# Delta-rule attention with two expert layers on one core: odd head pairs on the other half of the partitions, eight low weight parts offered to GpSimd, one chunk's turned keys in a gate tile

## The chip, the cores and the metric

The kernel runs on one core of a Trainium2 chip. What counts is the device time of one execution in microseconds (us), and of several executions the median. Engines are named as the profile names them: PE (TensorE, matrix products), PEld (its weight loads), DVE (VectorE), ACT (ScalarE), POOL (GpSimd) and SP (which starts the transfers).

## The reference

```python
# B, H, S, D = 4, 8, 768, 48
k_n = k / (norm(k, axis=-1) + 1e-6)
for t in range(S):                       # per batch and head, state is 48 x 48
    y[t] = q[t] @ state                  # read before the update
    v_old = k_n[t] @ state
    state = state + beta[t] * outer(k_n[t], v[t] - v_old)
x = y as (3072, 384)                     # 8 heads of 48 side by side
h = x @ w_in                             # 384 -> 2048
x = (h * sigmoid(1.702 * h)) @ w_out     # 2048 -> 384
p = domain_probs / (domain_probs.sum(-1) + 1e-9)
out = sum over e of p[:, e] * (relu(x @ w1[e]) @ w2[e])   # 4 experts, 384 -> 1024 -> 384
```

## The kernel before

**Attention.** The 768 tokens are cut into 12 chunks of 64 (u = 0 to 11). The 32 heads of all batches form 16 pairs (g = 0 to 15); x = 0 or 1 is the head in its pair. Of a pair, what lies by the feature sits on partitions `DR[x]` (0 and 64 on, 48 of each) and what lies by the token on `TR[x]` (64 and 0 on, 64 of each). A chunk takes these PE steps, each for all pairs: the key gram (L526 and L530, in `queue_g`), the query gram (L454, in `queue_q`), the old values `ks` (L750), two rounds of `solve` (L760) with a `cross` between (L774), the read of y (L791) and the state's update `write` (L813), the last five in `queue_chain`. A product in f32 stands in the profile as two matmuls, each with its weight load, so 32 products are 64 matmuls.

**Where products lie in the PE array.** Rows are chosen by the partitions of the operands, columns by those of the result. `ks`, both grams and `write` take their operands from one half of the partitions and leave the result on the other half: head x = 0 goes from rows 0 to columns 64, x = 1 from rows 64 to columns 0. `solve` stays on one 32 x 32 block of the diagonal, and four such blocks take turns. The pairs are worked in two halves (g 0 to 7, 8 to 15), each with a PSUM bank of its own (`ch0` and `ch1`, or two of `yg`, `ch0`, `ch1` for the grams, which the profile calls gp), one half after the other.

**Experts.** Tokens of two chunks form a tile of 512. Its first expert layer is L946 (into ph), then the gate on ACT and DVE, then L1043 (into px). The six tiles' first layers fill the PE between the steps of the attention; the second layer (L1170, L1200) follows when the attention is done. Tile 0 needs chunks u = 0 and 1; tile 1 is begun by halves, the first when y of u = 2 has been split (`split_x`, L940).

**What sets the order.** The class `Order` keeps a clock for each engine and a list of tasks with costs, dependencies and priorities. After each matmul of the experts it places the tasks that its clocks say are ready. So the order on every engine is fixed when the program is built, and a changed cost moves instructions. A task whose buffer is not free (`can`) waits; four scratch tiles (scr) are shared.

**Weights of the first layer.** Each of 16 blocks arrives as 64-bit numbers and is made 32-bit (`small` on ACT, `low` and `shift` on DVE), then split into a high part (`hi`, ACT) and a low part (`lo`, DVE, L285). GpSimd sets up masks and later computes the inverses (`queue_inverse`, L584 to L590).

**Turned keys.** Each chunk's keys are turned by DVE (L343) into a scratch tile and copied to kt by 8 copies (L181). For u = 3 the squares of the keys already stand in a tile of the gate's pool (two buffers).

Of the kernel before, what the change touches and what calls it, by code (L numbers as in the profile page):

```python
# [149 lines left out]
def delta_attention_moe_moe_kernel(  # L150
# [72 lines left out]

    def grid(t):
        return t[:, 0:NP * D].rearrange("p (g d) -> p g d", d=D)
# [18 lines left out]
    def queue_w1(f, after):  # L244
# [39 lines left out]
        def lo():  # L284
            nc.vector.tensor_tensor(out=W[f][:, 1, :], in0=cell["t"], in1=W[f][:, 0, :].bitcast(F32), op=ALU.subtract)  # L285
# [7 lines left out]
        wdone[f] = task(lo, "DVE", 0.95, (h,), **kw)  # L293
# [41 lines left out]
    def queue_turn(u, k2t, deps, p):  # L335
# [3 lines left out]
        def turn(h):  # L339
            if h == 0:  # L340
                b = claim(SCR, cell["end"])
                cell["t"] = scr[b][:, 0:NP * C].rearrange("p (h n i) -> p h n i", h=2, i=32)
            V.transpose(out=cell["t"][:, h], in_=k2t[:, 16 * h:16 * h + NP * D].rearrange(  # L343
                "p (g d) -> p g d", d=D)[:, :, 16 * h:16 * h + 32])
# [6 lines left out]
        a = task(lambda: turn(0), "DVE", 0.6, deps, prio=p, can=lambda: any_free(SCR))  # L351
# [80 lines left out]

    def queue_q(u):
# [11 lines left out]
        for g0 in range(0, NP, 8):  # L445
            cell = {}

            def gram(g0=g0, cell=cell):
                ps = cell["ps"] = psa.tile([128, 8, C], F32, name="gp", tag=claim(BANKS, cell["end"]))
                for i in range(8):  # L450
                    g = g0 + i
                    for x in range(2):
                        d = DR[x]
                        mm(ps[TR[x]:TR[x] + C, i, :], lhsT=kt[d:d + D, g, :], rhs=pq[d:d + D, g, x, :],  # L454
                           start=True, stop=True)

            def mask(x, g0=g0, cell=cell):
                r = TR[x]
                V.tensor_tensor(out=pq[r:r + C, g0:g0 + 8, x, :].rearrange("p (g o) i -> p g o i", o=2),
                                in0=cell["ps"][r:r + C].rearrange("p (g o) i -> p g o i", o=2),  # L460
                                in1=pmask[r:r + C].unsqueeze(1).broadcast_to([C, 4, 2, C]), op=ALU.mult)
# [3 lines left out]
            if len(visits) == whole:  # L465
                t = task(lambda fs=tuple(visits): [f() for f in fs], "PE", 1.0 * whole,
# [37 lines left out]
    def queue_g(u):  # L504
# [7 lines left out]
        for g0 in range(0, NP, 8):  # L512
            cell = {}

            def gram(g0=g0, cell=cell):
                ps = cell["ps"] = psa.tile([128, 8, C], F32, name="gp", tag=claim(BANKS, cell["end"]))
                if g0 == 0:
                    G[u] = ap_.tile([128, NP, SB], F32, name="g", tag="g", bufs=4)
                for i in range(8):
                    g = g0 + i  # L520
                    a, b = rows(g)
                    for x in range(2):
                        d, r = DR[x], TR[x] + a
                        for n, o in ((0, a), (SB, b)) if a else ((0, None),):
                            mv = kt[d:d + D, g, :] if o is None else kt[d:d + D, g, o:o + SB]
                            mm(ps[r:r + SB, i, n:n + mv.shape[1]], lhsT=kt[d:d + D, g, a:a + SB], rhs=mv,  # L526
                               start=True, stop=True)
                    for x in range(2):
                        d, r = DR[x], TR[x] + b
                        mm(ps[r:r + SB, i, 0:SB], lhsT=kt[d:d + D, g, b:b + SB], rhs=kt[d:d + D, g, b:b + SB],  # L530
                           start=True, stop=True)

            def keep_d(g0=g0, cell=cell):
                if w not in GG:
                    GG[w] = scr[claim(SCR, gheld[w]["end"])][:, 0:2 * NP * SB].rearrange("p (g i) -> p g i", i=SB)
                gg = GG[w][:, c * NP + g0:c * NP + g0 + 8, :]
                m = gg if w else cmask.unsqueeze(1).broadcast_to([128, 8, SB])
                V.tensor_tensor(out=gg, in0=cell["ps"][:, :, 0:SB], in1=m, op=ALU.mult)

            def keep_x(e, r, o, g0=g0, cell=cell):  # L540
                r += rows(o)[0]
                copy(e, G[u][r:r + SB, g0 + o:g0 + 8:2, :], cell["ps"][r:r + SB, o::2, SB:C])
# [4 lines left out]
            a = task(lambda fs=tuple(h[1] for h in halves): [f() for f in fs], "PE", 0.9 * whole,  # L547
                     (*placed[u], edone.get(u - 4), *diag[-1:]), prio=p, can=lambda: some_free(BANKS, whole))
            first = first or halves[0][0]
            for hc, _, kd, kx in halves:  # L550
                diag.append(task(kd, "DVE", 0.4, (a, premasked.get(w)), prio=p,
                                 can=None if w or u or hc is not first else lambda: any_free(SCR)))
                cross += [task(lambda e, r=r, o=o, kx=kx: kx(e, r, o), ("ACT", "DVE"), (0.24, 0.24), (a,), prio=p + 1)
                          for r in TR for o in range(2)]
                hc["end"] = (diag[-1], *cross[-4:])
# [148 lines left out]
    def queue_chain(u):  # L704
# [15 lines left out]
        def y_free():  # L720
# [6 lines left out]
            if u in YS:  # L727
                return at
# [3 lines left out]
        for hu in range(2):  # L732
            gs = slice(hu * HP, (hu + 1) * HP)
            cell = {}

            def each(gs=gs):
                for i, g in enumerate(range(gs.start, gs.stop)):
# [7 lines left out]
            def ks(take=take, each=each, cell=cell):  # L745
# [6 lines left out]
            def rest(gs=gs, cell=cell):  # L752
                V.tensor_tensor(out=V2[u][:, gs], in0=V2[u][:, gs], in1=cell["ps"], op=ALU.subtract)

            def solve(n, take=take, each=each, cell=cell):
                if u == 0 and n == 0:
                    take()
                for i, g, x in each():
                    r = TR[x] + rows(g)[n]
                    mm(cell["ps"][r:r + 32, i, :], lhsT=Tb[u][r:r + 32, g, :], rhs=V2[u][r:r + 32, g, :],  # L760
                       start=True, stop=True, tile_position=(r, r))

# [13 lines left out]

            def rest2(gs=gs, cell=cell):

                V.tensor_tensor(out=V2[u][:, gs], in0=V2[u][:, gs], in1=cell["ps"], op=ALU.subtract)

            def read(each=each, cell=cell):
                held["yg"] = cell["yev"]
                py = cell["py"] = psa.tile([128, HP, C], F32, name="y", tag="yg")
                for i, g, x in each():
# [6 lines left out]
                    mm(py[o:o + D, i, :], lhsT=SU[:, c0:c0 + D], rhs=pq[:, g, x, :], start=bool(t), stop=True)  # L791

# [17 lines left out]
            def write(each=each, cell=cell):  # L810
                for i, g, x in each():
                    o, r = DR[x], TR[x]
                    mm(cell["ps"][o:o + D, i, :], lhsT=k2[r:r + C, g, :], rhs=SUv[r:r + C, g, x, :],  # L813
                       start=True, stop=True)

            def y_copy(e, x, hu=hu, cell=cell):
                bs, at = slice(hu * B // 2, (hu + 1) * B // 2), slice(DR[x], DR[x] + D)
                src = cell["py"].rearrange("p (b m) i -> p m b i", m=4)[at]
                copy(e, xst[at, :, u % 2, bs, :], src[:, 0:KD])
                if u not in YS:  # L820
                    YS[u] = scr[claim(SCR, whole["end"])][:, 0:B * C].rearrange("p (b i) -> p b i", b=B)
                copy(e, YS[u][at, bs], src[:, KD])

            def s_add(x, gs=gs, cell=cell):
                o = DR[x]
                if u:
                    V.tensor_tensor(out=SUv[o:o + D, gs, x, :], in0=SUv[o:o + D, gs, x, :],
                                    in1=cell["ps"][o:o + D], op=ALU.add)
                else:
                    V.tensor_copy(out=SUv[o:o + D, gs, x, :], in_=cell["ps"][o:o + D])  # L830

            halves.append(dict(hu=hu, cell=cell, ks=ks, rest=rest, solve=solve, solved=solved, cross=cross, rest2=rest2,
# [4 lines left out]
        for hs in [halves[0:1], halves[1:2]] if u < 2 else [halves]:  # L837
            n = len(hs)

            def both(name, *args, hs=hs):  # L840
                return lambda: [h[name](*args) for h in hs]
# [12 lines left out]
            if u:  # L854
                a = task(both("ks"), "PE", 1.0 * n, (lv, invdone[u], *placed[u], *(hdone.get((u - 1, h["hu"])) for h in hs),
                                                      pdone[u] if n > 1 else None), prio=p, can=room)
                bs = [task(h["rest"], "DVE", 0.47, (a,), prio=p) for h in hs]
# [455 lines left out]
```

## Time and profile before

| | |
|---|---|
| median of 3 runs | 1443.52 us (1439.68 to 1447.65) |
| the profiled execution | 1446.42 us |
| its span, first to last instruction | 1444.7 us |
| PE busy | 1381.7 us, 96% |
| DVE, ACT, POOL busy | 641.5, 467.9, 191.4 us |

The profiled execution is 1.7 us longer than its span. Busy shares are means over stages with different limits: before about 74 us there is no expert work for PE, from there to 546 us attention and first layer share it, and after that only the experts run. A matmul's record lasts far longer than the distance to the next one, since matmuls overlap; a block's time is read from its first start to its last end.

### The profile page before, as it was taken

The numbers are of one execution on the slowest core, as the hardware profiler recorded it, in microseconds if no ns is written. First come the engines' busy times: TensorE is split into PE (matmuls) and PEld (weight loads), VectorE is DVE, ScalarE is ACT, GpSimd is POOL, SyncE is SP. The second block draws the span as 40 slices with busy tenths as digits, with TensorE's granted clock in tenths as the row PEclk, the third lists the DMA queues.
The fourth block names the chain that finished last, engine by engine and source line by source line (L and its number), as shares of the span: only waits on it lengthen the run. The fifth ranks groups of instructions, "written<-read, shape, count | busy, mean of one in ns | idle before, by whom it ended". The sixth has DMA issues, their size and how long they took to land.

```text
span 1444.7 us, 30526 instructions
## 1 busy us (share of the span) xinstructions
PE 1381.7 (96%) x13520; PEld 1170.7 (81%) x13520; DVE 641.5 (44%) x1068; ACT 467.9 (32%) x918; POOL 191.4 (13%) x346
## 2 busy tenths in 40 slices
PE   2699989999999999999999999999999999999999
PEld 2588789887777878887888888888888888888888
DVE  5989656565455232332333323443334333243333
ACT  5664535344344342432222212222112222121111
POOL 3048080184401700000000000000000000000000
PEclk9999989999999999999999999999999999999999
DMA  9311030200120010410010000100001110011111
GB/s 319 124 40 20 16 83 13 64 22 14 40 77 22 1 38 3 160 37 0 29 37 29 30 1 19 41 29 30 8 0 34 33 40 8 1 30 30 30 30 44
DMA packets 52164, 58.83 MB, mean 41 GB/s; under 512 B 36736, under 2 KB 38208, under 8 KB 52032
## 3 DMA queue, kind: packets, MB, share of 16 engines
q1 hardware_dynamic: 52032, 56.88, 13.2%
q8 instruction: 106, 1.74, 0.5%
q14 instruction: 26, 0.21, 0.0%
HBM read 47.96 MB, written 7.91 MB: 39 GB/s over the span
## 4 chain that ended last, share of the span: by engine, by line
PE 88%; DVE 4%; ACT 1%; issue 1%; DMA 1%; SPq 0%; DVEq 0%; ACTq 0%
PE ph L946 40%; PE po L1170 23%; PE px L1043 12%; PE po L1200 5%; PE y L791 2%; PE ch L750 1%; PE gp L454 1%; PE ch L760 1%; PE ch L813 1%; DMA pq<-in_q_dram 1%; PE gp L526 1%; ACT kt L181 1%; PE ch L774 1%; DVE gh L1061 0%; DVE w L285 0%
## 5 line engine op out<-in xcount | busy, mean ns | idle before, releaser
L946 PE MATMUL ph<-xs,w 128*128 128x512 f32 (+1 forms) x2808 | 656.9, 377 | 3.3 <-DVE xs L940 2.3
L946 PEld LDWEIGHTS ph<-xs,w 128*128 128x128 f32 x2808 | 503.4, 190 | 96.7 <-DVE xs L940 2.8
L1231 DVE SCALAR_TENSOR_TENSOR hh<-ph,hh 128x512 fp32r<-128x512 f32 x192 | 132.5, 690 | 503.4 <-ACT hh L1230 503.4
L1170 PE MATMUL po<-hh,w 128*128 128x512 f32 x1440 | 352.4, 389 | 0.0
L1170 PEld LDWEIGHTS po<-hh,w 128*128 128x128 f32 x1440 | 270.3, 188 | 56.1
L1230 ACT ACTIVATE hh<-ph 128x512 fp32r<-128x512 f32 x192 | 114.8, 598 | 616.8 <-PE ph L946 616.8
L1043 PE MATMUL px<-gh,w 128*128 128x512 f32 (+1 forms) x1080 | 235.6, 356 | 5.4 <-issue 3.0
L1043 PEld LDWEIGHTS px<-gh,w 128*128 128x128 f32 x1080 | 178.4, 192 | 34.6 <-issue 3.5
L1061 DVE TENSOR_TENSOR gh<-ph,gh 128x512 fp32r<-128x512 f32 (+1 forms) x120 | 69.7, 581 | 144.8 <-ACT gh L1060 143.9
L1058 ACT ACTIVATE ph<-ph 128x512 f32<-128x512 f32 (+1 forms) x120 | 59.6, 497 | 205.9 <-PE ph L946 203.1
L586 POOL TENSOR_TENSOR scr<-scr,itmp 128x30 f32<-128x30 f32 (+9 forms) x150 | 86.3, 576 | 11.8
L584 POOL TENSOR_TENSOR itmp<-scr 128x30 f32<-128x30 f32 (+9 forms) x150 | 81.3, 542 | 11.4
L1200 PE MATMUL po<-w,hh 128*128 128x384 f32 x384 | 73.9, 342 | 0.0
L1200 PEld LDWEIGHTS po<-w,hh 128*128 128x128 f32 x384 | 69.4, 188 | 2.4
L1060 ACT CAST gh<-ph 128x512 fp32r<-128x512 f32 (+1 forms) x120 | 60.1, 501 | 3.8
L526 PE MATMUL gp<-kt 48*32 48x32 f32 (+1 forms) x1152 | 27.7, 213 | 23.1 <-ACT kt L181 17.2
L526 PEld LDWEIGHTS gp<-kt 48*32 48x32 f32 x1152 | 24.6, 116 | 29.6 <-ACT kt L181 19.6
L181 ACT COPY su<-ch 64x384 f32<-64x384 f32 (+1 forms) x85 | 38.6, 458 | 25.1 <-PE ch L760 23.2
L1030 DVE TENSOR_TENSOR xs<-x,xs 128x512 fp32r<-128x512 f32 x72 | 45.2, 684 | 0.0
L181 ACT COPY kt<-scr 32x512 f32<-32x512 f32 (+1 forms) x63 | 38.9, 617 | 9.2 <-DVE scr L343 8.2
L1029 ACT CAST xs<-x 128x512 fp32r<-128x512 f32 x72 | 39.7, 619 | 0.0
L454 PE MATMUL gp<-pq,kt 48*64 48x64 f32 x768 | 30.8, 240 | 8.6 <-DMA pq<-in_q_dram 5.8
(118 smaller groups left out, 876.4 us busy)
## 6 DMA issues: line engine op xcount, KB each, us to landing
raw<-in_we_dram SPq DMA_DIRECT2D x32, 384.0 KB, 3.0
rw<-in_w_dram SPq DMA_DIRECT2D x14, 768.0 KB, 12.1
raw<-prd SPq DMA_DIRECT2D x20, 256.0 KB, 3.2
k<-in_k_dram SPq DMA_DIRECT2D x12, 384.0 KB, 4.8
pq<-in_q_dram SPq DMA_DIRECT2D x24, 192.0 KB, 4.4
v<-in_v_dram SPq DMA_DIRECT2D x12, 384.0 KB, 3.3
out_dram<-oacc SPq DMA_DIRECT2D x80, 48.0 KB, 1.7
x1d<-raw SPq DMA_DIRECT2D x12, 256.0 KB, 2.1
```

Of the source, the lines that this page charges most:

```text
L181: (nc.scalar.copy if e == "ACT" else nc.vector.tensor_copy)(out=out_, in_=in_)
L526: mm(ps[r:r + SB, i, n:n + mv.shape[1]], lhsT=kt[d:d + D, g, a:a + SB], rhs=mv, start=True, stop=True)
L584: E.tensor_tensor(out=tv, in0=x[:, j:j + 1, j + 1:].broadcast_to([128, m, r]), in1=x[:, 0:m, j:j + 1].broadcast_to([128, m, r]), op=ALU.mult)
L586: E.tensor_tensor(out=x[:, 0:m, j + 1:], in0=x[:, 0:m, j + 1:], in1=tv, op=ALU.add)
L946: mm(ps, lhsT=w[:, a, kk * 128:(kk + 1) * 128], rhs=xs[kk][:, b, cs], start=kk == 0 and i == 0, stop=kk == KD - 1 and i == 2)
L1043: mm(px[d][:, cs], lhsT=w[:, a, 384 + d * 128:384 + (d + 1) * 128], rhs=gh[:, b, 0:cs.stop - cs.start], start=f == 0 and i == 0 and cs.sta ...
L1060: a = task(lambda: nc.scalar.copy(out=hi, in_=ph), "ACT", 0.05 + 0.43 * c, (a,), **kw)
L1061: a = task(lambda: nc.vector.tensor_tensor(out=lo, in0=ph, in1=hi.bitcast(F32), op=ALU.subtract), "DVE", 0.07 + 0.53 * c, (a,), **kw)
L1170: mm(po[kk], lhsT=w[:, a, 384 + kk * 128:384 + (kk + 1) * 128], rhs=hh[:, c, :], start=f == 0 and i == 0, stop=f == F2 - 1 and i == 2)
L1200: mm(ps, lhsT=hh[:, a, b * 128:(b + 1) * 128], rhs=w[:, c, 384:768].rearrange("p (k a i) -> p a k i", a=4, k=KD), start=f == 0 and i == 0, ...
L1230: nc.scalar.activation(out=hh[:, 0, :], in_=ph, func=AF.Relu)
L1231: nc.vector.scalar_tensor_tensor(out=hh[:, 1, :], in0=ph, scalar=0.0, in1=hh[:, 0, :].bitcast(F32), op0=ALU.max, op1=ALU.subtract)
```

## The change

Pairs are now dealt to the two halves by parity: half 0 has the even pairs, half 1 the odd ones. In the gram steps from u = 2 (queries) and u = 4 (keys), and in `ks` and `write` from u = 2, the odd pairs' results go to the other half of the columns (`half`, `flip`): rows 0 to columns 0, rows 64 to columns 64. `weave` issues the halves alternately, product by product. The readers of those results take them from the other partitions; where one instruction covered both heads of a half, the odd half now needs two (`rest`, `keep_d`). The key gram takes one product of 64 columns for every pair, where odd pairs had two of 32. The copies of its cross part are 4 of 256 elements a chunk, where 8 of 128 stood, and y is copied by 6 instructions, where 8 stood. `lo` of weight blocks 0 to 7 may go to POOL or DVE. The turned keys of u = 3 take a gate tile. Costs in the planner follow.

```diff
+    def half(x, flip):
+        return DR[x] if flip else TR[x]
...
-        def lo():
-            nc.vector.tensor_tensor(out=W[f][:, 1, :], in0=cell["t"], in1=W[f][:, 0, :].bitcast(F32), op=ALU.subtract)
+        def lo(e="DVE"):
+            (nc.gpsimd if e == "POOL" else nc.vector).tensor_tensor(
+                out=W[f][:, 1, :], in0=cell["t"], in1=W[f][:, 0, :].bitcast(F32), op=ALU.subtract)
...
-        wdone[f] = task(lo, "DVE", 0.95, (h,), **kw)
+        wdone[f] = (task(lo, ("POOL", "DVE"), (1.9, 1.0), (h,), **kw) if f < N_EARLY else
+                    task(lo, "DVE", 1.0, (h,), **kw))
...
+                if u == 3:
+                    t = ghp.tile([128, 2, TT], F32R, name="gh", tag="gh").rearrange("p h c -> p (h c)").bitcast(F32)
+                else:
+                    t = scr[claim(SCR, cell["end"])]
...
+    def weave(fs):
+        for _ in zip(*(f() for f in fs)):
+            pass
...
-                t = task(lambda fs=tuple(visits): [f() for f in fs], "PE", 1.0 * whole,
+                t = task(lambda fs=tuple(visits): weave(fs), "PE", 1.0 if whole == 1 else 1.3,
...
+                        d, r = DR[x], half(x, flip) + a
+                        mm(ps[r:r + SB, i, :], lhsT=kt[d:d + D, g, a:a + SB], rhs=kt[d:d + D, g, :], start=True, stop=True)
+                        yield
...
-            gs = slice(hu * HP, (hu + 1) * HP)
+            gs = slice(hu, NP, 2) if t else slice(hu * HP, (hu + 1) * HP)
+            flip = t and hu
...
-                    d, r = DR[x], TR[x]
+                    d, r = DR[x], half(x, flip)
                     mm(ps[r:r + C, i, :], lhsT=kt[d:d + D, g, :], rhs=SUv[d:d + D, g, x, :], start=True, stop=True)
+                    yield
...
-                    o, r = DR[x], TR[x]
+                    r, o = TR[x], half(1 - x, flip)
                     mm(cell["ps"][o:o + D, i, :], lhsT=k2[r:r + C, g, :], rhs=SUv[r:r + C, g, x, :],
                        start=True, stop=True)
+                    yield
...
-                return lambda: [h[name](*args) for h in hs]
+                return lambda: weave([lambda h=h: h[name](*args) for h in hs])
...
-                bs = [task(h["rest"], "DVE", 0.47, (a,), prio=p) for h in hs]
+                bs = [task(lambda h=h, x=x: h["rest"](x), "DVE", 0.47, (a,), prio=p)
+                      for h in hs for x in (range(2) if t and h["hu"] else (None,))]
```

On PE, before, `ks` of u = 3 stands behind the key gram of u = 5, ahead of the first matmuls of tile 1 (ph of 256 columns); the two numbers of ch are the two halves' banks:

```order
L526 MATMUL gp<-kt_75 32x32 x4
L530 MATMUL gp<-kt_75 32x32 x2
L750 MATMUL ch_2774<-su,kt_77 64x48 x16
L750 MATMUL ch_2791<-su,kt_77 64x48 x16
L946 MATMUL ph<-xs,w 128x256 x9
L1043 MATMUL px_1227<-gh,w 128x512
```

Of the changed kernel on PE, the second read of u = 2 with what follows it, `ks` of u = 3 (L769):

```order
L1070 MATMUL px_1134<-gh,w 128x512
L1070 MATMUL px_1135<-gh,w 128x512 x3
L812 MATMUL y<-pq_78,su 48x64 x16
L769 MATMUL ch_2694<-su,kt_77 64x48
L769 MATMUL ch_2696<-su,kt_77 64x48
L769 MATMUL ch_2694<-su,kt_77 64x48
L769 MATMUL ch_2696<-su,kt_77 64x48
L769 MATMUL ch_2694<-su,kt_77 64x48
```

The two banks now alternate product by product. Counted along PE, the second read of u = 2 stood behind 416 matmuls of the experts and now stands behind 423, which are all that tile 0 has at that point; the key gram of u = 5, once behind that read, now stands ahead of `ks` of u = 2. Its place between the read and tile 1 is taken by `ks` of u = 3 and its first `solve` (32 products).

The key gram of u = 4 on PE, before (gp and its number are the bank):

```order
L526 MATMUL gp_2277<-kt0_74 32x64 x2
L530 MATMUL gp_2277<-kt0_74 32x32 x2
L526 MATMUL gp_2277<-kt0_74 32x32 x4
L530 MATMUL gp_2277<-kt0_74 32x32 x2
L526 MATMUL gp_2277<-kt0_74 32x64 x2
```

and in the changed kernel:

```order
L538 MATMUL gp_2177<-kt0_74 32x64
L538 MATMUL gp_2180<-kt0_74 32x64
L538 MATMUL gp_2177<-kt0_74 32x64
L538 MATMUL gp_2180<-kt0_74 32x64
L542 MATMUL gp_2177<-kt0_74 32x32
L542 MATMUL gp_2180<-kt0_74 32x32
```

Ten products for two pairs became eight, in two banks by turns, so that 160 matmuls are 128.

On POOL, before, the first inverse follows the masks directly:

```order
L979 AFFINE_SELECT pmask<-scr_100 32x64 x8
L981 MEMSET pq_79 128x2048
L578 MEMSET scr_100 128x32
L584 TENSOR_TENSOR itmp<-scr_100 128x30
L586 TENSOR_TENSOR scr_100<-scr_100,itmp 128x30
```

and in the changed kernel:

```order
L1006 AFFINE_SELECT pmask<-scr_100 32x64 x8
L1008 MEMSET pq_79 128x2048
L289 TENSOR_TENSOR w<-raw,w 128x768
L289 TENSOR_TENSOR w<-rw,w 128x768 x4
L596 MEMSET scr_101 128x32
L602 TENSOR_TENSOR itmp<-scr_101 128x30
```

Five of the eight low parts went to POOL, between the masks and the first inverse; the other three stayed on DVE.

## Rows read from the trace of the kernel before

**Rows 1.** The page: busy time by engine, fetched instructions, chain that ended last.

```profile
PE 1381.7 (96%) x13520; PEld 1170.7 (81%) x13520; DVE 641.5 (44%) x1068; ACT 467.9 (32%) x918; POOL 191.4 (13%) x346
...
q8 instruction: 106, 1.74, 0.5%
...
PE 88%; DVE 4%; ACT 1%; issue 1%; DMA 1%; SPq 0%; DVEq 0%; ACTq 0%
```

**Rows 2.** Busy time by stretch: us, engines (instructions), granted clock, DMA share, GB/s.

```profile
40.00:60.00 20.00, 13.17 (x605) 12.03 (x606) 19.25 (x37) 10.17 (x19) 0.00 (x0) 1.00 0.31 121
...
74.00:182.00 108.00, 103.05 (x1977) 89.56 (x1976) 87.75 (x143) 60.34 (x138) 47.76 (x68) 0.99 0.11 26
182.00:546.00 364.00, 349.66 (x6128) 297.97 (x6129) 183.56 (x334) 153.19 (x344) 132.51 (x244) 0.97 0.13 37
```

**Rows 3.** Timeline of PE, and chain, around the start of tile 1.

```profile
172.61 1.10 PE L791 MATMUL y<-pq,su 128*48 128x64 f32 x32
173.64 1.88 PE L1043 MATMUL px<-gh,w 128*128 128x512 f32 x7
...
180.17 0.39 PE L946 MATMUL ph<-xs,w 128*128 128x256 f32 x1
181.95 2.07 PE L946 MATMUL ph<-xs,w 128*128 128x256 f32 x8 [1.40 <-DVE xs L940]
...
177.07 3.49 DMA stage<-scr
```

**Rows 4.** Timeline of PE: start, us from first start to last end, matmuls.

```profile
236.74 2.07 PE L750 MATMUL ch<-su,kt 48*64 48x48 f32 x64
...
240.73 0.88 PE L760 MATMUL ch<-v,scr 32*32 32x48 f32 x64
...
248.84 1.64 PE L813 MATMUL ch<-su,k 64*48 64x48 f32 x64
...
275.05 2.08 PE L454 MATMUL gp<-pq,kt 48*64 48x64 f32 x64
```

**Rows 5.** Groups of PE by shape, 182 to 546 us: busy us, mean ns of one.

```profile
L750 PE MATMUL ch<-su,kt 48*64 48x48 f32 x512 | 16.5, 219 | 0.0
```

**Rows 6.** Groups of PE, 456.4 to 458.5 us: one key gram.

```profile
L530 PE MATMUL gp<-kt 48*32 48x32 f32 x64 | 1.8, 197 | 0.0
L526 PE MATMUL gp<-kt 48*32 48x32 f32 x64 | 1.7, 194 | 0.0
L526 PE MATMUL gp<-kt 48*32 48x64 f32 x32 | 1.7, 219 | 0.0
```

**Rows 7.** Timeline of DVE: the second subtraction after `ks`, and two low parts.

```profile
238.86 0.56 DVE L753 TENSOR_TENSOR v<-v,ch 128x384 f32<-128x384 f32 x1 [0.38 <-PE ch L750]
...
48.20 0.94 DVE L285 TENSOR_TENSOR w<-raw,w 128x768 fp32r<-128x768 f32 x1
...
52.59 0.94 DVE L285 TENSOR_TENSOR w<-rw,w 128x768 fp32r<-128x768 f32 x1
```

**Rows 8.** Two-input operations on POOL; key copies and first gate on ACT.

```profile
L590 POOL TENSOR_TENSOR scr<-scr,bt 128x1024 f32<-128x1024 f32 x5 | 9.7, 1937 | 0.4
...
L491 POOL TENSOR_TENSOR scr<-gmask,bt x1: 2511/2511/2511, 431.6 to 431.6; 128x1024 f32<-128x1024 f32 x1
...
69.13 4.39 ACT L181 COPY kt<-scr 32x512 f32<-32x512 f32 x7
...
77.41 0.37 ACT L1058 ACTIVATE ph<-ph 128x256 f32<-128x256 f32 x1
```

**Rows 9.** What PE waited for, 74 to 546 us: us, times, longest.

```profile
PE gp L454 <- DMA pq<-in_q_dram: 5.8, 5, 1.8
...
PE gp L530 <- issue: 2.1, 1, 2.1
```

**Rows 10.** Stretches of low clock, the first and the last of five.

```profile
180.90:187.70 6.80, 5.75 (x78) 4.81 (x79) 3.34 (x8) 3.27 (x8) 5.77 (x14) 0.50 0.58 119
...
327.60:334.50 6.90, 5.46 (x33) 4.34 (x33) 4.62 (x8) 3.14 (x8) 0.00 (x0) 0.51 0.01 2
```

More of the change, by code (lines that the diff above doesn't have):

```diff
@@ L444, in queue_q, with gram, mask @@
         whole = 1 if u < 2 else 2
-        for g0 in range(0, NP, 8):
+        for o in range(2):
             cell = {}
-            def gram(g0=g0, cell=cell):
+            flip = o and whole == 2
+            def gram(o=o, cell=cell, flip=flip):
                 ps = cell["ps"] = psa.tile([128, 8, C], F32, name="gp", tag=claim(BANKS, cell["end"]))
                 for i in range(8):
-                    g = g0 + i
                     for x in range(2):
[L453 to L461, printed above, removed]
+                        d, r, g = DR[x], half(x, flip), 2 * i + o
+                        mm(ps[r:r + C, i, :], lhsT=kt[d:d + D, g, :], rhs=pq[d:d + D, g, x, :], start=True, stop=True)
+                        yield
+            def mask(x, o=o, cell=cell, flip=flip):
+                r, s = TR[x], half(x, flip)
+                V.tensor_tensor(out=pq[r:r + C, o::2, x, :], in0=cell["ps"][s:s + C],
+                                in1=pmask[r:r + C, o].unsqueeze(1).broadcast_to([C, 8, C]), op=ALU.mult)
             visits.append(gram)
@@ L511, in queue_g, with gram @@
         whole = 1 if u < 4 else 2
-        for g0 in range(0, NP, 8):
+        for o in range(2):
             cell = {}
-            def gram(g0=g0, cell=cell):
+            flip = o and whole == 2
+            def gram(o=o, cell=cell, flip=flip):
                 ps = cell["ps"] = psa.tile([128, 8, C], F32, name="gp", tag=claim(BANKS, cell["end"]))
-                if g0 == 0:
+                if not o:
                     G[u] = ap_.tile([128, NP, SB], F32, name="g", tag="g", bufs=4)
+                a, b = rows(o)
@@ L534, in keep_d @@
                 if w not in GG:
                     GG[w] = scr[claim(SCR, gheld[w]["end"])][:, 0:2 * NP * SB].rearrange("p (g i) -> p g i", i=SB)
[L536 to L542, printed above, removed]
+                a = rows(o)[0]
@@ new lines, in keep_d, with keep_x @@
+                r, n = (0, 128) if x is None else (TR[x], C)
+                s = 0 if x is None else half(x, flip)
+                gg = GG[w][r:r + n, c * NP + o:(c + 1) * NP:2, :]
+                m = gg if w else cmask[r:r + n].unsqueeze(1).broadcast_to([n, 8, SB])
+                V.tensor_tensor(out=gg, in0=cell["ps"][s:s + n, :, a:a + SB], in1=m, op=ALU.mult)
+            def keep_x(e, x, o=o, cell=cell, flip=flip):
+                a, b = rows(o)
+                r, s = TR[x] + a, half(x, flip) + a
+                copy(e, G[u][r:r + SB, o::2, :], cell["ps"][s:s + SB, :, b:b + SB])
@@ L546, in queue_g @@
                 continue
-            a = task(lambda fs=tuple(h[1] for h in halves): [f() for f in fs], "PE", 0.9 * whole,
+            a = task(lambda fs=tuple(h[1] for h in halves): weave(fs), "PE", 0.9 if whole == 1 else 1.4,
                      (*placed[u], edone.get(u - 4), *diag[-1:]), prio=p, can=lambda: some_free(BANKS, whole))
@@ L550, in queue_g @@
             for hc, _, kd, kx in halves:
[L551 to L555, printed above, removed]
+                parts = range(2) if whole == 2 and hc is not first else (None,)
+                diag += [task(lambda kd=kd, x=x: kd(x), "DVE", 0.4, (a, premasked.get(w)), prio=p,
+                              can=None if w or u or hc is not first else lambda: any_free(SCR)) for x in parts]
+                cross += [task(lambda e, x=x, kx=kx: kx(e, x), ("ACT", "DVE"), (0.3, 0.33), (a,), prio=p + 1)
+                          for x in range(2)]
+                hc["end"] = (*diag[-len(parts):], *cross[-2:])
             halves.clear()
```

78 lines of the change are left out of this document (40 added, 38 removed).

## The prediction

> **What bounds the kernel now.** I read the page first: PE is busy for 96% of the span and carries 88% of the chain that ended last [rows 1]. Then the stretches: from 74 us on PE has work nearly all the time (103 of 108 us, then 350 of 364) at a granted clock of 0.97 or more, while DVE, ACT and POOL have gaps [rows 2]. So from there to 546 us a microsecond of PE work taken away is a microsecond of time, unless a wait takes its place. Behind 546 us nothing changes. Ahead of 74 us DVE leads: it is busy for 19.25 of the 20 us from 40 to 60 [rows 2].
>
> One wait belongs to the structure. The second read of u = 2 ends at 172.61 + 1.10 = 173.71 us, and the first full run of tile 1's matmuls starts at 181.95, 8.24 us later: the copies, a transfer of 3.49 us and the split on DVE lie between, and PE had nothing left of tile 0 [rows 3]. Up to there a saving counts only as far as that read comes earlier; the 8.24 us stay.
>
> **The steps that get shorter.** A `ks` takes 2.07 us for 64 matmuls whose records last 0.22 us each [rows 4, 5], so (2.07 - 0.22) / 63 = 29.4 ns from one to the next. The query gram has the same pace, `write` (1.64 - 0.21) / 63 = 22.7 ns, and `solve`, on four blocks of the array by turns, (0.88 - 0.20) / 63 = 10.8 ns [rows 4]. The first three have two places in the array, from rows 0 to columns 64 and the reverse. The change gives them four. No row shows what four do for such tiles: from below the pace cannot be taken under solve's 10.8 ns, from above nothing is gained (29.4). What separates the two is whether places that share rows, or share columns, run at once. Sharing rows is shown: the key gram sends each row half to two column strips, and its 160 matmuls take 1.8 us, 10 ns each [rows 6]. Sharing columns between two row halves is in no row; but the two results go to two banks. I take half of today's pace, that is, each place keeps its own: 14.7 and 11.4 ns. `ks` and the query gram then save 0.93 us each, `write` 0.72.
>
> A rule of the Trainium skill speaks against this, in "TensorE: Matmul & The Clock Gate", Part 3, The mechanism: a weight load overlaps a running matmul only if it goes to another row group. By it a flipped pair, which shares its rows with its even neighbour, would load only behind that neighbour's matmul, and the saving of these three steps would be nothing instead of 0.93 and 0.72. The key gram of [rows 6] has such neighbours and runs at the solve's pace, so here the trace is against the rule; no row has them with 64 columns.
>
> The key gram has 128 matmuls instead of 160. At its own 10 ns that saves 0.3 us from u = 4 on; with u = 2 and 3, not flipped, I count nothing.
>
> **Up to the start of tile 1.** Start: the low parts of blocks 0 and 1, 0.94 us each at 48.20 and 52.59 [rows 7], leave a DVE that had no gap: -1.9 (ends 0 and -4, since the steps behind are placed anew). Then, ahead of the second read of u = 2: two query grams -1.9, `ks` -0.9, `write` -0.7, key gram of u = 4 -0.3. Against that the key gram of u = 5 now stands ahead of it (128 at 10 ns and one record, +1.5), and seven more matmuls of the experts, which took 1.88 us [rows 3]. Sum -2.3, so the read ends near 171.4 and tile 1 starts near 179.6. Inside the 8.24 us PE did a key gram and a `ks`; now it does a `ks` (1.14), waits for three subtractions (1.7) and does a `solve` (0.88), then stands for some 4.5 us. The `solve` is work done earlier, -0.9. **Together -3.2.**
>
> **Behind it**, where PE is never short of expert work: `ks` of u = 4 to 11, 8 x 0.93 = 7.4; query grams of the same, 7.4; `write` of u = 3 to 11, 9 x 0.72 = 6.5; key grams of u = 6 to 11, 6 x 0.3 = 1.8. **Together -23.1.**
>
> **What it adds.** The subtraction behind `ks` becomes three DVE instructions. Today the second ends at 238.86 + 0.56, 2.68 us behind the start of `ks` [rows 4, 7]: the first runs beside the second half of the block. Woven, all three wait for its end: 1.14 + 3 x 0.56 + 0.1 = 2.9 us. `solve` is queued behind them on PE; its cover is the expert matmuls placed between, 8 or more. I take +0.2 for ten chunks, **+2** (ends 0, and 5 if a gate instruction of DVE comes first half the time). The extra masks and the fewer, longer copies fall to engines that are idle half the time [rows 2]: nothing, unless DVE has no gap. The five low parts on POOL: its two-input operations of 1024 elements took 1.94 and 2.51 us [rows 8], three quarters of that is 1.5 to 1.9; at the dearer, 9.5 us on an engine with nothing else to do before the first inverse. Block 0 is not needed until tile 0 begins near 74 us, some 23 us later. If POOL were not done when the inverse is ready, that inverse, `ks` of u = 2 and tile 1 would all start later by as much. The gate tile for u = 3: the key copies end at 69.13 + 4.39 = 73.5, the first gate runs at 77.41 [rows 8]; 3.9 us of cover, nothing.
>
> **Sum:** -3.2 - 23.1 + 2 = -24.3 us. Against the profiled execution that is 1446.4 - 24.3 = 1422; that execution lay 2.9 us over the median of the three runs, so for a median I say **1419 us** (-1.7%).
>
> **Rivals.** *No gain from four places* (0.08). Places with common columns, or common rows, take turns after all. For: no row of before has common columns; the rule above. Against: [rows 6] for rows. What stays is the start, the key grams and the new waits: -1.9 - 2.1 + 2 = -2, so about 1441.5 us, no difference that this measurement can tell (0.5%, 7 us, is about its limit).
>
> *Instructions come too slowly* (0.12). The page counts 106 fetches for PE; 27,040 matmuls and loads over 106 is 255 in one, 127 matmuls with their loads [rows 1]. The longest wait in which the profile shows nothing waited for, 2.1 us, stands inside a key gram, the densest block of all [rows 9]. Denser blocks could run into it more often. Against: 3 of 4 such blocks have 64 matmuls and expert matmuls around them. If half of the gain behind tile 1 were lost so, 11.5 us: about 1430 us. The Trainium skill ("Runtime: NRT & Kernel Launch", Instruction fetch mechanics) has blocks of 256 instructions and calls the crossing mostly hidden; the 255 agrees, and by its second part this rival costs nothing, which the 2.1 us speak against.
>
> *Slower: changing the row half under the same columns drains the array* (0.05). Place: every flipped `ks`, query gram and `write`. If a matmul waited for the whole record (219 ns [rows 5]) of the one with its columns, two at a time would give 110 ns per matmul and 7.1 us for a `ks` instead of 2.07, +5 on each of some 30 blocks, 1590 us. It decides from the point where the pace passes today's 29.4 ns (22.7 for `write`) by 1 ns, which over 30 x 64 matmuls eats the 2 us that the rest brings; slower by 7 us takes some 5 ns.
>
> **Chances.** The forecast's case has 0.75. Its own range: with the pace of `solve` the three steps give 5 us more; the start may give 2 more, and if the waits of [rows 9] and the stretches of half clock that follow such waits (five, the first 6.8 us and the last 6.9 at 1.2 GHz, of which half is lost [rows 10]) become fewer, 5 more: 1407. Upward, 3 of waits and 2 of the start: 1424. To leave out no more than 2 in 10 the range reaches through the second rival: 1407 to 1434. Faster by over 0.5% (under 1436): 0.75 + 0.12 = 0.87; within 0.5%: 0.08; slower: 0.05.
>
> **What would show it.** In the timeline of PE: `ks` and query gram near 1.15 us, `write` near 0.93, a key gram near 1.5; near 2.1 and 1.6 the first rival is right, above that the third. First matmuls of tile 1 near 179.6, with a wait for DVE's split of some 4.5 us ahead of them. Waits put down to "issue" inside the woven blocks would be the second rival. Blocks 0 to 4 with 1.5 to 1.9 us on POOL. The prediction is wrong if the chain behind `ks` makes PE wait by more than half a microsecond a chunk, or if the inverse of u = 2 and 3 ends later and carries tile 1 with it.

## The result, and the profile after

The changed kernel takes 1421.11 us (median of 4 runs, 1419.33 to 1423.71), the kernel before 1445.59 in the same comparison; the ratio is 0.9845, with a 95% interval of 0.9807 to 0.9884. The prediction of 1419 us was 2 us off. (One run of before, of 1959.68 us, was disturbed: it is in that median and not in the ratio; the median of the other three is 1443.52.) So the medians lie 22.4 us apart. The profiled execution took 1421.22 us, its span 1419.5, which is 25.2 us less than before; the sum had said 24.3.

The page, as in [rows 1]:

```profile
PE 1356.2 (96%) x13136; PEld 1144.7 (81%) x13136; DVE 654.1 (46%) x1081; ACT 455.1 (32%) x850; POOL 198.9 (14%) x351
...
q8 instruction: 103, 1.69, 0.5%
```

The stretches, as in [rows 2], the last one from where tile 1's first run begins. It ends at 546 us as there, though the attention's last matmul is now at 519.8 us (545.3 before), so it holds some 25 us more of the experts alone:

```profile
40.00:60.00 20.00, 13.42 (x634) 12.38 (x638) 18.39 (x34) 9.69 (x18) 3.71 (x2) 1.00 0.31 116
74.00:185.00 111.00, 100.51 (x1927) 86.32 (x1926) 90.95 (x147) 54.81 (x115) 69.24 (x105) 0.97 0.10 24
185.00:546.00 361.00, 351.09 (x5985) 295.32 (x5986) 198.82 (x352) 153.89 (x318) 114.62 (x210) 0.97 0.13 37
```

And the longest waits of PE in the last of them, as in [rows 9]:

```profile
PE gp L468 <- DMA pq<-in_q_dram: 4.2, 6, 1.6
PE px L1070 <- issue: 3.1, 1, 3.1
PE gp L538 <- ACT gh L1087: 1.2, 1, 1.2
```

The time did not go where the sum put it. Tile 1 starts at 184.98 us instead of 181.95, so 3.0 us were **lost** up to there, where 2.3 were to be won; and from there to the end it is 1419.5 - 184.98 = 1234.5 us instead of 1444.7 - 181.95 = 1262.8, which is 28.2 less, where the forecast comes to 22.0 (23.1 and 0.9 for the solve done earlier, less 2 of new waits). The two errors, 5.3 and 6.2 us, have opposite signs; that the total came so close is luck.

The timeline of PE around one chunk, the answer to [rows 4] (start, us from first start to last end, matmuls):

```profile
235.24 1.15 PE L769 MATMUL ch<-su,kt 48*64 48x48 f32 x64
...
238.67 0.88 PE L783 MATMUL ch<-v,scr 32*32 32x48 f32 x64
...
248.24 0.94 PE L835 MATMUL ch<-su,k 64*48 64x48 f32 x64
...
256.96 1.16 PE L468 MATMUL gp<-pq,kt 48*64 48x64 f32 x64
```

`ks`, `write` and the query gram last 1.15, 0.94 and 1.16 us; 1.15, 0.93 and 1.15 had been forecast, from 2.07, 1.64 and 2.08. (1.15 - 0.22) / 63 is 14.8 ns. These are blocks without a wait inside and at full clock; others are longer (query grams up to 2.03 us, `ks` up to 1.60). The seven whole key grams last 1.63 to 2.31 us, not the 1.5 that was said to show it.

The start of tile 1 in the timelines of PE, ACT and DVE; compare [rows 3]:

```profile
175.10 1.10 PE L812 MATMUL y<-pq,su 128*48 128x64 f32 x32
176.13 0.31 PE L769 MATMUL ch<-su,kt 48*64 48x48 f32 x2
179.00 1.71 PE L769 MATMUL ch<-su,kt 48*64 48x48 f32 x62 [2.56 <-DVE su L853]
181.34 0.36 PE L783 MATMUL ch<-v,scr 32*32 32x48 f32 x2 [0.63 <-DVE v L776]
182.49 1.50 PE L783 MATMUL ch<-v,scr 32*32 32x48 f32 x62 [0.79 <-DVE v L776]
184.98 2.32 PE L973 MATMUL ph<-xs,w 128*128 128x256 f32 x8 [0.99 <-ACT xs L181]
...
184.02 0.47 ACT L181 COPY su<-ch 64x384 f32<-64x384 f32 x1 [7.12 <-PE ch L783]
184.52 0.71 ACT L181 CAST xs<-stage 128x256 fp32r<-128x256 f32 x2
...
180.73 1.70 DVE L776 TENSOR_TENSOR v<-v,ch 128x384 f32<-128x384 f32 x3 [1.88 <-PE ch L769]
182.84 0.71 DVE L181 CAST xs<-stage 128x256 fp32r<-128x256 f32 x1 [0.41 <-DVE v L776]
```

And the transfer there, in the chain:

```profile
179.45 2.41 DMA stage<-scr
```

The read ends at 176.20 us (175.10 + 1.10; 171.4 was forecast), and tile 1 starts 8.78 us behind it, not 8.24. The transfer has landed at 181.86. But on DVE the three subtractions end only at 182.43, and on ACT the splits of tile 1 stand behind a copy that waits for `solve` (184.02). `ks`, from which this chain hangs, waited 2.56 us for the state's update of u = 2.

### The profile page after: what moved, and what is told of

Its sections match the earlier page's. It is cut to its first block, busy times and chain, and to the rows that moved or that the text cites. A ratio compares the mean times of both kernels' runs of the same rounds, so it can differ in the third digit from the quotient of the medians.

```text
span 1419.5 us, 29692 instructions
## 1 busy us (share of the span) xinstructions
PE 1356.2 (96%) x13136; PEld 1144.7 (81%) x13136; DVE 654.1 (46%) x1081; ACT 455.1 (32%) x850; POOL 198.9 (14%) x351
## 4 chain that ended last, share of the span: by engine, by line
PE 88%; DVE 6%; ACT 2%; issue 2%; DMA 1%; SPq 0%; DVEq 0%
PE ph L973 40%; PE po L1197 23%; PE px L1070 13%; PE po L1227 5%; PE y L812 2%; PE ch L783 1%; ACT kt L181 1%; PE gp L538 1%; DMA pq<-in_q_dram 1%; PE ch L769 1%; PE ch L798 1%; PE gp L468 1%; DVE pq L473 1%; PE ch L835 1%; DVE w L289 0%
## 5 line engine op out<-in xcount | busy, mean ns | idle before, releaser
L538 PE MATMUL gp<-kt 48*32 48x64 f32 x768 | 25.9, 238 | 19.3 <-ACT kt L181 17.8
L181 ACT COPY kt<-scr 32x512 f32<-32x512 f32 (+1 forms) x56 | 34.6, 618 | 11.1 <-DVE scr L352 10.3
L473 DVE TENSOR_TENSOR pq<-gp,pmask 64x512 f32<-64x512 f32 x48 | 33.0, 688 | 8.6 <-PE gp L468 7.6
```

Source lines behind the costliest of these rows:

```text
L181: (nc.scalar.copy if e == "ACT" else nc.vector.tensor_copy)(out=out_, in_=in_)
L538: mm(ps[r:r + SB, i, :], lhsT=kt[d:d + D, g, a:a + SB], rhs=kt[d:d + D, g, :], start=True, stop=True)
```

## The experiments

Every ratio is against the kernel before, timed beside it on the same chip. Different runs come from different chips; the median of before lies between 1443.5 and 1447.0 us on them, so a difference of one or two us between two runs is not clear of noise.

**1. Two places.** Half 1 back on the even pairs' columns; all order and all readers as changed.

```diff
-        return DR[x] if flip else TR[x]
+        return TR[x]
```

> The changed kernel with the odd pairs' results back on the even pairs' columns (two places in the array, as before), everything else as changed: deal by parity, halves woven, two banks by turns, three subtractions. Theory (each place keeps its own pace of 29.4 ns, four places halve it): ks and query gram go back to 2.07 us, write to 1.64, the key gram stays; 10 x 0.92 + 10 x 0.93 + 10 x 0.71 = 25.6 us, about 1446 us. Rival (it is the two banks by turns, or the weaving, that halves the pace): blocks stay at 1.15 and 0.93 us, 1421 us.

1439.79 us, ratio 0.9963 (0.9946 to 0.998).

**2. Halves in turn.** Four places, but half 1 issued behind half 0.

```diff
+    def in_turn(fs):
+        for f in fs:
+            for _ in f():
+                pass
...
-                t = task(lambda fs=tuple(visits): weave(fs), "PE",
+                t = task(lambda fs=tuple(visits): in_turn(fs), "PE",
...
+                run = in_turn if name in ("ks", "write") else weave
```

> The changed kernel with four places, but ks, query gram and write issued one half after the other, so that only two places are in use at a time. Theory (places overlap only when their products stand next to each other): the three blocks go back to 2.07 and 1.64 us, about 1446 us, as with two places. Rival (a straight place, rows 0 to columns 0, is quicker in itself than a crossed one): only the second half of each block is quicker, ks near 1.6 us, about 1433 us.

1435.56 us, ratio 0.9937 (0.9922 to 0.9952).

**3. Rows apart.** `weave` takes two products of a half, then two of the other, so the order of places, rows to columns, is 0 to 64, 64 to 0, 0 to 0, 64 to 64.

```diff
-        for _ in zip(*(f() for f in fs)):
-            pass
+        its = [f() for f in fs]
+        live = True
+        while live:
+            for it in its:
+                for _ in range(2):
+                    live = next(it, its) is not its
```

> The changed kernel woven two products at a time, so that neighbours never share rows (in the changed kernel every second neighbour does); all else as changed. Theory (each place keeps its own pace, whatever its neighbour): ks stays at 1.15 us and the time at 1421 us. Rival (a weight load waits for a running matmul in the same rows): today's pace still holds such waits; without them ks, query gram and write near the pace of solve, 0.9 us, 0.25 us less in 30 blocks, about 1414 us.

1421.63 us, ratio 0.9839 (0.9824 to 0.9853).

One `ks` of each of the three runs in turn, in the timeline of PE:

```profile
241.98 2.10 PE L769 MATMUL ch<-su,kt 48*64 48x48 f32 x64
```

```profile
236.67 1.88 PE L774 MATMUL ch<-su,kt 48*64 48x48 f32 x64
```

```profile
234.25 1.15 PE L773 MATMUL ch<-su,kt 48*64 48x48 f32 x64
```

With two places, banks by turns give nothing: the blocks are back at 2.10 and 1.68 us, and the rival of run 1 falls. With the halves in turn, 1.88 us is much nearer to 2.07 than to 1.15; the straight half (rows 0 to columns 0) is not quicker in itself (its matmuls start 26.2 ns apart in that block, those of the crossed half 27.3). Sharing rows with the neighbour costs nothing: the order of run 3 avoids it and changes neither block nor time.

The starts of single records show how. Of before, a `ks` starts a matmul after 7 ns, the next after 52, and so on; of the changed kernel after 7, 7, 6 and 38. So two matmuls start in every 58 or 59 ns (45 for `write`) with two places, and four with four. Read as one matmul from each place, that means that each place keeps its own pace, as the forecast's middle value supposed; the records do not name their place. The times rose by 18.7 and 14.5 us where 25 were expected: the blocks grew, but other stalls shrank (in run 1 the wait for queries from 4.2 to 2.4 us, the time at half clock from 24 us to 17).

**4. Low parts on DVE alone.** The planner places the rest anew. (The expectations call the order that the planner gives the instructions its places; these are not the places in the array.)

```diff
-        wdone[f] = (task(lo, ("POOL", "DVE"), (1.9, 1.0), (h,), **kw) if f < N_EARLY else
-                    task(lo, "DVE", 1.0, (h,), **kw))
+        wdone[f] = task(lo, "DVE", 1.0, (h,), **kw)
```

> The changed kernel with all low parts on the vector engine, as before; the planner places the rest anew. The prediction's term: the two parts of 0.94 us come back to an engine without a gap, so tile 0 and the end are 1.9 us later, about 1423 us. Rival (the trace after: the first full run of tile 0 starts at 73.73 us, where 73.79 stood before, because the vector engine then waits for products and takes another weight block earlier): nothing comes back, tile 0 near 73.7 us and 1421 us.

1417.83 us, ratio 0.9814 (0.9799 to 0.9828): neither; it is 3.3 us **faster** than the changed kernel, and 3.8 faster than run 3, which was timed beside it. Its timeline of PE at the start of tile 1:

```profile
169.59 1.10 PE L811 MATMUL y<-pq,su 128*48 128x64 f32 x32 [0.54 <-DVE stage L181]
...
175.43 1.96 PE L768 MATMUL ch<-su,kt 48*64 48x48 f32 x64 [1.33 <-ACT g L181]
177.32 0.58 PE L972 MATMUL ph<-xs,w 128*128 128x256 f32 x1
179.43 2.08 PE L972 MATMUL ph<-xs,w 128*128 128x256 f32 x8 [1.54 <-DVE xs L966]
```

Here the read comes 5.5 us earlier and tile 1 starts at 179.43 us, which is what had been forecast for the changed kernel (179.6). Behind the read stand the key gram of u = 5 and `ks`, no `solve`. (PE's granted clock was 0.50 from 40 to 60 us in this trace; tile 0 starts no later for it, at 72.98 us.) Two causes are possible, GpSimd itself or the planner's order; the next four runs part them.

**5. Same order, other engine.** The changed kernel's order, every low part executed by DVE.

```diff
-            (nc.gpsimd if e == "POOL" else nc.vector).tensor_tensor(
+            nc.vector.tensor_tensor(
```

> The changed kernel with every instruction in the place the planner gave it, but the five low parts that went to GpSimd run on the vector engine, at those places. Prediction's term: an engine without a gap gets five parts of 0.94 us, of which two ahead of tile 0: 2 us later at tile 0 and 4.7 us by tile 1, 1423 to 1426 us. Rival (beside GpSimd the vector engine's two-input work takes longer, which eats what it is spared): 1421 us, and its mean times fall.

1424.97 us, ratio 0.9854 (0.9827 to 0.9881). First full run of tile 0, then of tile 1, in its timeline of PE:

```profile
76.15 2.30 PE L973 MATMUL ph<-xs,w 128*128 128x256 f32 x17 [0.84 <-DVE xs L829]
...
189.56 2.50 PE L973 MATMUL ph<-xs,w 128*128 128x256 f32 x8 [0.99 <-ACT xs L181]
```

The changed kernel has 73.73 and 184.98. So with the same order GpSimd's share **is** worth something: 2.4 us at tile 0, 4.6 at tile 1, 3.9 between the medians. But 0.8 us of it stand in the traces already at the `shift` of block 0 (45.24 against 46.04 us), ahead of any low part, so 1.6 are left at tile 0, where 1.9 had been forecast. The two medians come from two chips, and the ratios, 0.9845 and 0.9854, differ by less than their intervals.

**6. and 7. The same pair on the kernel before.** Its `lo` offered to GpSimd as in the changed kernel (the `lo` lines of the diff, nothing else), and then this order with every part on DVE.

> The kernel before with nothing changed but the low parts of blocks 0 to 7 offered to GpSimd at the changed kernel's costs; the planner places the rest anew. Prediction's term: two low parts off an engine without a gap, 1.9 us less, 1443.5 us. Theory from the run with all low parts on the vector engine (it was 3.3 us faster than the changed kernel): the vector engine's two-input work slows beside GpSimd's, and the planner's new places cost more than the parts give; no gain, 1445 to 1449 us.

> The kernel before with the planner's places of the run in which its low parts were offered to GpSimd (1439.9 us, 7 us faster than before), but all low parts run on the vector engine. If GpSimd's share made those 7 us: back to 1445 to 1447 us. If the new places made them: 1440 to 1442 us.

1439.90 us, ratio 0.9949 (0.9929 to 0.9969), and 1444.13, ratio 0.9986 (0.9967 to 1.0005). So run 6's theory fell: on the kernel before, the offer brings 7 us. By the medians GpSimd's share makes 4.2 of them; what the new order makes, 2.7, is not clear of noise. First full run of tile 1 in run 6's timeline of PE:

```profile
185.85 2.08 PE L948 MATMUL ph<-xs,w 128*128 128x256 f32 x8 [1.11 <-DVE xs L942]
```

Run 6 starts tile 1 earlier than run 7 (189.14), but 3.9 us later than the kernel before (181.95). In its trace the 7 us are won behind that point (1437.4 - 185.85 = 1251.6 us to the end, where before has 1262.8), not by a shorter start, as the prediction's term would have it.

**8. The hand-over held.** In the changed kernel the key gram of u = 5 is kept back until the second read of u = 2, and the first `solve` of u = 3 until tile 1 has begun.

```diff
-                     (*placed[u], edone.get(u - 4), *diag[-1:]), prio=p, can=lambda: some_free(BANKS, whole))
+                     (*placed[u], edone.get(u - 4), *diag[-1:], read2[2] if u == 5 else None), prio=p, can=lambda: some_free(BANKS, whole))
...
-prio=p, can=None if u else room)
+prio=p,
+                     can=room if not u else (lambda: 0.0 if od.second else None) if u == 3 else None)
```

> The changed kernel with two things held back around the start of tile 1: the key gram of u = 5 until the second read of u = 2, and the first solve of u = 3 until tile 1 has begun; so that PE's order there is that of the kernel before; low parts stay on GpSimd. Theory (the order at that place made tile 1 late: 184.98 us where 179.6 were forecast): the read ends 2 us earlier, the splits no longer stand behind solve's copies, tile 1 starts near 181 us; one solve and one key gram are not moved out of the rest, so about 1417 us. Rival (it is the low parts on GpSimd, which slow the first tile, that cost the 3.3 us found): tile 1 stays behind 183 us, 1421 us.

1419.18 us, ratio 0.981 (0.9783 to 0.9837). The timeline of PE:

```profile
172.33 1.10 PE L813 MATMUL y<-pq,su 128*48 128x64 f32 x32
...
179.70 0.58 PE L976 MATMUL ph<-xs,w 128*128 128x256 f32 x1 [0.53 <-ACT xs L182]
182.02 2.08 PE L976 MATMUL ph<-xs,w 128*128 128x256 f32 x8 [1.74 <-DVE xs L970]
```

The read is 2.8 us earlier and tile 1 begins with one matmul at 179.70 and runs from 182.02, 3.0 us earlier with low parts still on GpSimd: the order at this place was that much of the loss. In the end 1.9 us remain, which is not clear of noise: from there to the end run 8 takes 1418.1 - 182.02 = 1236.1 us instead of 1234.5, with a `solve` and a key gram to do later. The other 2.7 us by which run 4 reads earlier are won ahead of the read, 0.9 of them by tile 0 (72.98 against 73.90); what wins the rest is not shown.

**9. Turned keys of u = 3 in scratch.**

```diff
-                if u == 3:
-                    t = ghp.tile([128, 2, TT], F32R, name="gh", tag="gh").rearrange("p h c -> p (h c)").bitcast(F32)
-                else:
-                    t = scr[claim(SCR, cell["end"])]
+                t = scr[claim(SCR, cell["end"])]
```

> The changed kernel with the turned keys of u = 3 in a scratch tile again; the planner places the rest anew. Prediction: the gate tile neither costs nor brings anything, 1421 us. Rival (the scratch tile frees something that the start waits for): the key copies of u = 3 come later, and tile 0 with them, 2 to 4 us, 1424 us.

1420.83 us, ratio 0.9818 (0.9798 to 0.9837): the gate tile neither costs nor brings anything.

**10. Query tile by head.** A load then writes 4 KB in one piece to a partition.

```diff
-    PQ = [ap_.tile([128, NP, 2, C], F32, name=f"pq{i}") for i in range(2)]
+    PQ = [ap_.tile([128, 2, NP, C], F32, name=f"pq{i}") for i in range(2)]
...
-                nc.sync.dma_start(out=pq[DR[x]:DR[x] + D, :, x, :], in_=q[u, x])
+                nc.sync.dma_start(out=pq[DR[x]:DR[x] + D, x], in_=q[u, x])
```

> The changed kernel with the query tile laid out by head first, so that a load writes 4 KB in one piece to a partition where it wrote sixteen pieces of 256 bytes; the order of all instructions is the same. In the profile after, PE waited 4.2 us for these loads (six times, 1.6 us at most), they took 4.4 us each, and one fetch of instructions stood behind them and the keys: 3.3 us without work at 262.7 and then 10 us at half clock. Theory (the small pieces make the loads long, and the fetch waits behind them): load near 3 us, waits for it under 1 us, the stall at 262.7 shorter; 1413 to 1418 us. Rival (the load is long because it shares the engines with the keys, whatever its pieces, and a fetch is late because it is asked for late): waits stay, 1421 us.

1416.21 us, ratio 0.9782 (0.9758 to 0.9806). The page's row of the load:

```profile
pq<-in_q_dram SPq DMA_DIRECT2D x24, 192.0 KB, 3.4
```

The waits of PE from 185 to 546 us:

```profile
PE px L1070 <- issue: 2.3, 1, 2.3
...
PE gp L468 <- DMA pq<-in_q_dram: 1.3, 1, 1.3
```

The load takes 3.4 us instead of 4.4, PE waits for it once instead of six times (1.3 us instead of 4.2), and the wait for instructions shrinks from 3.1 to 2.3 but stays. The execution profiled here, 1419.42 us, is the slowest of the four, so these rows stand for less than the 4.9 us between the medians; run 9, timed beside it, took 1420.83.

**11. and 12. Together.** Run 4 with the query tile by head; then the same order with the low parts of blocks 0 to 4 on GpSimd.

```diff
-            (nc.gpsimd if e == "POOL" else nc.vector).tensor_tensor(
+            (nc.gpsimd if f < 5 else nc.vector).tensor_tensor(
```

> The changed kernel with all low parts on the vector engine and the query tile laid out by head. If the two edits act on different waits they add up: 1417.8 us less what the query layout alone gives the changed kernel, 1410 to 1414 us. If the layout gives nothing: 1418 us.

> The version with the query tile laid out by head and the planner's places for low parts on the vector engine (1412.67 us), with every instruction in its place, but the low parts of blocks 0 to 4, which start between 47 and 82 us there, run on GpSimd, ahead of its first inverse. Theory (at the same places GpSimd's share is worth 3.9 to 4.2 us, as the two pairs of runs with equal places showed): about 1409 us. Rival (these places were made for a vector engine that does the parts, and a part on GpSimd is ready 0.9 us later, or the first inverse is): no gain, 1412 to 1414 us.

1412.67 us, ratio 0.9759 (0.9738 to 0.9779), and 1411.80, ratio 0.9764 (0.974 to 0.9788). Run 11 adds up (1417.83 - 4.9 = 1412.9) and beats both kernels. Run 12 gains nothing: its tile 0 starts at 73.25 us instead of 71.03, because DVE, freed, now waits for PE's products (2.2 us in two waits, where 0.4 in one stood) and 1.6 us for nothing that the profile shows.

## Why the prediction was right, and where it was not

**The shorter steps: right.** Behind tile 1 the busy time of `ks` fell from 16.5 to 9.8 us, of the query gram from 18.7 to 11.7, of `write` from 14.8 to 8.4: 6.7 + 7.0 + 6.4 = 20.1 us where 7.4 + 7.4 + 6.5 = 21.3 had been forecast. The groups of PE, two of before (from 182 us; for `ks` see [rows 5]) and three of the changed kernel (from 185 us):

```profile
L454 PE MATMUL gp<-pq,kt 48*64 48x64 f32 x512 | 18.7, 227 | 5.8 <-DMA pq<-in_q_dram 5.8
...
L813 PE MATMUL ch<-su,k 64*48 64x48 f32 x576 | 14.8, 206 | 0.0
```

```profile
L468 PE MATMUL gp<-pq,kt 48*64 48x64 f32 x512 | 11.7, 234 | 4.2 <-DMA pq<-in_q_dram 4.2
...
L769 PE MATMUL ch<-su,kt 48*64 48x48 f32 x512 | 9.8, 221 | 0.2 <-issue 0.2
...
L835 PE MATMUL ch<-su,k 64*48 64x48 f32 x576 | 8.4, 207 | 0.0
```

Half of today's pace was the right choice between 10.8 and 29.4 ns, and runs 1 to 3 show that it is the places that make it. *No gain from four places* and *draining* are refuted. The Trainium skill ("TensorE: Matmul & The Clock Gate", Part 3, The mechanism) says, in its list of what overlaps, that a weight load overlaps a running matmul only in another row group; by it the changed kernel's blocks, where every second neighbour shares its rows, would have stayed at 2.07 us, and run 3 would have been quicker. The traces have 1.15 us for both. (The key grams, with fewer matmuls, gave 2.3 us of busy time, 12.8 to 10.5, where 1.8 had been forecast.)

**Up to the start of tile 1: wrong.** This is the step that failed, -2.3 us as the prediction put it and +3.0 as measured. Three parts of it. (a) The start: -1.9 was forecast, and the first full run of tile 0 moved from 73.79 in the trace of before to 73.73. The two low parts did leave DVE, but what that spared, 1.88 us, was used up there. The `shift` of block 1 ran beside GpSimd's first low part and took 1.88 us instead of 0.94 (the last section has the rows). And the planner gave DVE five of the key copies ahead of tile 0, where it had given it three (2.14 us instead of 1.27). One of the five:

```profile
71.35 0.42 DVE L181 COPY kt<-gh 16x512 f32<-16x512 f32 x1
```

-1.88 + 0.94 + 0.87 is as good as nothing. Waits do not explain it, nor a weight block taken earlier, as the rival of run 4 has it (four `shift`s stand ahead of tile 0 in both): DVE, to which the prediction gave no gap, waited 2.2 us from 30 to 74 us before, mostly for a key copy on ACT, and 2.0 now, for PE. First before, then the changed kernel:

```profile
DVE scr L692 <- ACT kt L181: 1.9, 1, 1.9
```

```profile
DVE scr L710 <- PE gp L705: 1.2, 1, 1.2
DVE v L776 <- PE ch L798: 0.8, 1, 0.8
```

With the same order there is a saving (run 5); but the order that the planner chooses when it is offered GpSimd cost 7.1 us more than that of run 4 (1424.97 against 1417.83, both with every part on DVE, on two chips; 5.8 by the ratios), and GpSimd gives back 3.9 of them. (b) The order ahead of the read: the key gram of u = 5, which took 2.31 us where 1.5 had been counted, and more waits for the gate in tile 0 (3.3 us where 2.2 stood). (c) The 8.24 us, which became 8.78: I let PE do `ks` at once, then wait for the subtractions; but `ks` was held for the update of the state, and I did not look at what `solve`'s copies stand ahead of on ACT. Run 8 gives 3.0 us of (b) and (c) back.

**New waits: +2 forecast.** Behind tile 1 none is seen at `solve`; the planner puts enough of the experts' work between. The price fell in the hand-over (1.4 us there), and in a place I had not named: `cross` is woven too, so its first products of half 1 wait for a copy that half 0 used to hide. Its busy time rose from 7.9 to 9.1 us: two of the nine blocks waited so (1.29 us instead of 0.88), and a third, 1.50 us, ran at half clock.

**Fewer stalls: inside the range, not in the sum.** The rows of waits behind tile 1 add up to 10.6 us instead of 15.5; without the one that ends where tile 1 begins (1.0 and 1.4) it is 9.6 instead of 14.1. That accounts for most of what was won beyond the sum: 20.1 of blocks, 2.3 of key grams, 4.5 of waits and 1.2 of `solve`, less 1.2 of `cross`, are 26.9 of the 28.2 us; the other 1.3 I have not parted. Each figure is of one execution, and those of before lay up to 8 us apart (1439.68 to 1447.65), so how much of the fewer waits is the change's is not shown. The time at half clock did not fall: three stretches, 24 us together, where five made 24. Windows of the clock (us, engines, granted clock, DMA share, GB/s):

```profile
179.30:189.60 10.30, 7.88 (x196) 6.74 (x189) 5.04 (x9) 3.77 (x8) 9.20 (x15) 0.50 0.41 89
209.80:213.30 3.50, 3.50 (x19) 3.50 (x19) 1.34 (x3) 1.49 (x3) 0.00 (x0) 0.54 0.00 0
264.60:274.80 10.20, 8.70 (x94) 8.36 (x95) 4.63 (x6) 0.76 (x3) 7.29 (x19) 0.50 0.01 2
```

**Instructions come too slowly: present, at one place.** In the timeline of PE, behind a key gram:

```profile
262.33 0.62 PE L1070 MATMUL px<-gh,w 128*128 128x256 f32 x3
266.10 1.65 PE L1070 MATMUL px<-gh,w 128*128 128x256 f32 x6 [3.15 <-issue]
```

Inside the woven blocks there are 0.2 us of such waits. With the half clock behind this one (1.2 GHz for 10.2 us, of which half is lost) it costs some 8 us, an estimate, but the kernel before had four such waits, 6.5 us together, and the half clock behind two of them. A fetch of instructions arrived at 264.8 us, behind queries and keys that filled the DMA engines until then; run 10, with quicker loads, shortens the wait by 0.8 us. Each of the five waits, four before and this one, ends 1.3 to 1.7 us after a fetch of 16 KB has landed. That the fetch is late for this reason alone is not shown: waits of the kind stand in the kernel before without such traffic. ("Runtime: NRT & Kernel Launch" in the Trainium skill, Instruction fetch mechanics, calls the crossing mostly hidden; the 3.15 us are the exception here.)

**GpSimd's parts** last 1.85 to 1.88 us, at the dear end of what was said; **the gate tile** is worth nothing (run 9).

## What to carry to other kernels

Small products run at a pace of each place in the array; spread them over every pair of row half and column half and issue the places by turns, and the pace divides by their number, whichever neighbours share rows or columns. That is shown here for f32 products of 48 rows by 64 columns and of 64 by 48, with two places and with four. Where a planner sets the order, an offer of a second engine is two changes: run the new order with the old engine to part them, since here the engine brought some 4 us and in the changed kernel the order took more. A hand-over with nothing to cover it is to be read on all engines, copies of the next step included, since what is placed into the gap can stand ahead of what ends it.

## What the runs showed of the hardware

An operation of DVE with two inputs can stand still beside one of GpSimd. The `shift` of a weight block (128 x 768) in the changed kernel, first beside a low part on POOL, then with none beside it:

```profile
47.23 1.85 POOL L289 TENSOR_TENSOR w<-raw,w 128x768 fp32r<-128x768 f32 x1 [34.79 <-ACT w L286]
```

```profile
48.02 1.88 DVE L281 SCALAR_TENSOR_TENSOR rw<-rw 128x768 int32<-128x768 int32 x1
...
70.35 0.96 DVE L281 SCALAR_TENSOR_TENSOR rw<-rw 128x768 int32<-128x768 int32 x1
```

The first ends at 49.90 us, 0.82 behind the low part (49.08), and lasts twice as long as the second. It happens once more: a low part runs from 82.27 to 84.14, and the `shift` that starts at 82.45 lasts 2.51 us and ends 0.82 behind it. In run 5, which has no low parts on GpSimd, the first of them takes 0.94. Other work of DVE beside low parts kept its time: the query masks, which read PSUM (0.69 and 0.68 us), and reductions with one input (0.94). So of the 4.7 us that five parts on GpSimd spare DVE, 2.5 (0.94 and 1.57) are lost again in two instructions.

And pieces of 256 bytes make a load of 192 KB last 4.4 us where pieces of 4 KB take 3.4.
